# A chunked state-space scan: two heads' M and x in one product, and another order of the turn

## The chip, the cores and the metric

The kernel runs on one core of a Trainium2 chip. The metric is the device time of one execution in microseconds (us). Three executions of the kernel before took 242.53, 243.75 and 241.89, so the median is 242.53.

## The reference

Two blocks follow each other. The first is a Mamba-2 scan over 4 batches, 8 heads and 768 positions, with 32 columns of x a head and a state of 16 x 32. The second sends each of the 3072 tokens to one of 8 experts by a hash of its id.

```python
for c in range(nc):                       # chunks of 32 positions
    L = np.exp(cum[:, :, :, None] - cum[:, :, None, :]) * causal
    M = np.einsum('bhin,bhjn->bhij', Cc, Bc) * L
    y_intra = np.einsum('bhij,bhjd->bhid', M, xc)
    y_inter = np.einsum('bhin,bhnd->bhid', Cc, state) * decay_to_i[:, :, :, None]
    y[:, :, sl] = y_intra + y_inter
    state = decay_full[:, :, None, None] * state + np.sum(Bx, axis=2)
...
x = y.transpose(0, 2, 1, 3).reshape(3072, 256)
for e in range(8):
    out[e's tokens] = np.maximum(x[e's tokens] @ w1[e], 0.0) @ w2[e]
```

The result does not depend on the size of a chunk. The kernel uses chunks of 64.

## The kernel before, in words

**The scan.** The 3072 positions are cut into 12 pairs of 128-position tiles (three pairs a batch, `PB`). Each tile holds two chunks of 64, `u`. A loop (`for k in range(-1, NP)`, L724) runs one *turn* per pair, and works on three pairs at once: it finishes pair k, makes the products of pair k + 1 and prepares pair k + 2. Every engine executes its instructions in exactly the order in which the program writes them; there is no planner (`manual_schedule`, L85), and engines wait for each other by semaphores. The pieces of a turn are:

- `turn_bc` and `evict_bc` (L214, L225): TensorE transposes a third of the next batch's B and C, scaled by the decays, and ScalarE copies the transposes to SBUF as `bt`, `ce` (C, split into even and odd heads) and `ct`. A batch is ready after three turns; the last part of C is turned in turns 1, 4 and 7, and the `gram` of those same turns reads it.
- `back` and `evict_back` (L520, L526): B of pair k + 2 is transposed back, and copied to `bn`.
- `gram` (L566): C times B for each head, chunk and tile of pair k + 2. Each product covers a 32-row, 64-column part of the TensorE array.
- `masked` (L578): VectorE copies the causal half of it to `m_sb`, in two instructions of 128x512.
- `intra` (L611): M times x for pair k + 1, one product for each of 8 heads, 2 tiles and 2 chunks. M of 64x64 is the stationary operand, x of two heads (64 columns) the moving one, and half of each result isn't used. The results go to the PSUM banks `BY` and `BY + 1`. A tiny ScalarE copy, `seen`, follows them.
- `dstates` and `states` (L530, L543): B times x gives each chunk's addition to the state; VectorE chains them as `z`, and GpSimd scales each into `sp`.
- `inter` (L591): C times the state, added to intra's results of pair k in PSUM; then ScalarE evicts y to `y_sb`, and `y_store` (L626) writes it to DRAM.

TensorE's order in a turn is: `turn_bc`, `back`, `inter(k)`, `gram(k + 2)`, `intra(k + 1)`, `dstates(k + 2)`. ScalarE's is: first evictions of B and C, y of pair k, `bn`, the other evictions, `seen`.

**The routing**, in pieces beside the scan (`piece`, L675), finds out which token goes to which slot of an expert. Its last steps need one-hot rows of each tile's lanes (`rt_lanes`, L403): VectorE makes some in a few wide instructions, GpSimd makes the others one by one. In turn 8 TensorE multiplies them into a table (`rt_table`, L419), from which the index lists come.

**The seam.** After the scan GpSimd gathers the tokens' rows in tiles of 128 (`gather`, L474). Tiles 0 to 6 (`EK`) hold only tokens from the first 2048, and are asked for early (`ASK`, L718); the others need all of y in DRAM. `turn_x` (L482) transposes a gathered tile. The experts' products then start with those that need only early tiles: 16 `up` groups of four matmuls (L984 to L1004), between which tiles are turned. In `step(0)` (L1025) follow the other products of expert 0, for which VectorE makes sums and differences of quarters of the matrices (`sum_w1`, `sum_w2`, `sums_x`, L803 to L825), since each expert's product is done with seven products of quarters in place of eight. From there on, to the end, TensorE goes through the eight experts.

Trace records: an fp32 matmul of the program shows as two records on PE and two weight loads on PEld.

Of the kernel before, what the change touches and what calls it, by code (L numbers as in the profile page):

```python
# [25 lines left out]
def kernel(  # L26
# [113 lines left out]
    m_sb = [awork.tile([P, 2, G, 2 * T], F32, name=f"m{i}", bufs=1) for i in range(2)]  # L140
# [4 lines left out]
    cmask = apre.tile([P, 2, T], F32)  # L145
    pool_e.memset(cmask, 1.0)
    for u in range(2):
        pool_e.affine_select(out=cmask[u * T:(u + 1) * T], in_=cmask[u * T:(u + 1) * T], pattern=[[0, 2], [1, T]],
                             compare_op=OP.is_ge, fill=0.0, base=0, channel_multiplier=-1)
# [380 lines left out]
    def dstates(k, bank=0, half=1):  # L530

        b, j = divmod(k, PB)
        for t in range(2):
            for hh in range(2):
                for u in range(2):
                    if j == PB - 1 and t == 1 and u == 1:
                        continue
                    pe.matmul(out=ps[hh * T:(hh + 1) * T, bank + u, half * 2 * P + t * P:half * 2 * P + (t + 1) * P],  # L538
                              lhsT=bns[k][u * T:(u + 1) * T, t, hh * T:(hh + 1) * T],
                              rhs=xs[2 * k + t][u * T:(u + 1) * T, 4 * hh:4 * hh + 4].rearrange("q h d -> q (h d)"),  # L540
                              start=True, stop=True, skip_group_check=True)

    def states(k, ns, bank=0, half=1):  # L543
# [4 lines left out]
        for n in ns:  # L548
# [10 lines left out]
            d = ps[:, bank + u, half * 2 * P + t * P:half * 2 * P + (t + 1) * P]  # L559
# [4 lines left out]
            zs["z"] = z  # L564

    def gram(k):  # L566
        b, j = divmod(k, PB)
        for gs in ((2, 3), (0, 1)):
            for t in range(2):
                for u in range(2):  # L570
                    c = (2 * j + t) * P + u * T
                    for g in gs:
                        r = slice(32 * g, 32 * g + 32)
                        pe.matmul(out=ps[u * T:(u + 1) * T, g, t * P:(t + 1) * P].rearrange("q (e i) -> q e i", e=2),  # L574
# [3 lines left out]
    def masked(k, half):  # L578
        m = m_sb[k % 2]
        mk = cmask.bitcast(I32).rearrange("q e i -> q (e i)").unsqueeze(1).unsqueeze(1).to_broadcast([P, 2, 2, 2 * T])  # L580
        g = slice(2 * half, 2 * half + 2)
        dve.copy_predicated(out=m[:, :, g], mask=mk, data=ps[:, g, 0:2 * P].rearrange("q g (t s) -> q t g s", t=2))  # L582

    def y_own(r, u):

        v = ps[r, BY + u].rearrange("q (t g b d) -> q t g b d", t=2, g=2, d=D)
        return v[:, :, :, 0:4:3]
# [3 lines left out]
    def inter(k):  # L591
# [3 lines left out]
        for u in range(2):  # L595
            for t in range(2):
# [4 lines left out]
                for hh in range(2):  # L601
                    r = slice(hh * T, (hh + 1) * T)
                    pe.matmul(out=y_own(r, u)[:, t], lhsT=cts[b][r, c:c + T], rhs=sps[k][r, n], start=False, stop=True,  # L603
                              skip_group_check=True)
            o = ysb[k].rearrange("q t u (g e d) -> q u t g e d", g=2, e=2)
            if k == NP - 1 and u:
                dve.tensor_copy(out=o[:, u], in_=y_own(slice(0, P), u))
            else:
                act.activation(o[:, u], y_own(slice(0, P), u), AF.Copy)

    def intra(k):  # L611
        for t in range(2):
            for h4 in range(4):
                for u in range(2):
                    for hh in range(2):
                        h = hh * 4 + h4
                        o = ps[hh * T:(hh + 1) * T, BY + u, (t * 4 + h4) * 2 * D:(t * 4 + h4 + 1) * 2 * D]
                        pe.matmul(out=o, lhsT=m_sb[k % 2][u * T:(u + 1) * T, t, h // 2, (h % 2) * T:(h % 2 + 1) * T],  # L618
                                  rhs=xs[2 * k + t][u * T:(u + 1) * T, h // 2 * 2:h // 2 * 2 + 2],
                                  start=t == 0 and h4 == 0, stop=False, skip_group_check=True)  # L620
# [54 lines left out]
    def piece(k):  # L675
# [20 lines left out]
        elif k == 6:  # L696
            rt_tiles()
            rt_lanes(0, 4, dve)
            rt_lanes(15, 18, pool_e)
        elif k == 7:  # L700
            rt_lanes(4, 11, dve)
            rt_lanes(18, NCH, pool_e)
# [15 lines left out]
    ASK = {8: EK[:2], NP - 2: EK[2:-1]}  # L718
# [5 lines left out]
    for k in range(-1, NP):  # L724
# [12 lines left out]
        tb, qb, sb = (BY + 1, BY, BT) if k == -1 else (BT, BQ, 0)  # L737
        if bt_ < NB:
# [11 lines left out]
        if k == NP - 2:  # L750
            for i, q in enumerate(AHEAD):
                turn_x(q, (BQ, BT)[i % 2])
        if k >= 0:
            inter(k)
# [20 lines left out]
        if k == 7:  # L775
            rt_lanes(11, 15, dve)
# [4 lines left out]
        if k == NP - 2:  # L781

            passed = apre.tile([P, 2, 1], F32)
# [34 lines left out]
    def sums_x(p):  # L818
        n = HALF[p]
        q = lambda k, j: xT[:, k, slots(p, j)]  # L820
        t = t1[p] = mwork.tile([P, 4, N0], F32, name="t1")
        dve.tensor_tensor(out=t[:, 0, 0:n], in0=q(0, 1), in1=q(0, 0), op=OP.subtract)  # L822
        dve.tensor_tensor(out=t[:, 1, 0:n], in0=q(1, 1), in1=t[:, 0, 0:n], op=OP.subtract)
        dve.tensor_tensor(out=t[:, 2, 0:n], in0=q(0, 1), in1=q(1, 1), op=OP.subtract)
        dve.tensor_tensor(out=t[:, 3, 0:n], in0=q(1, 0), in1=t[:, 1, 0:n], op=OP.subtract)  # L825
# [153 lines left out]
    ask(2)  # L979
    gather(EK[-1], early=True)  # L980
    ask(4)
    turns = [k for k in EK if k not in turned] + turn_due(0)
    n = 0
    for p in range(NEAR):  # L984
        for what in (1, 2):
            for q0 in (0, 2):
                up(p, q0, what, (0, 1, 2, BT)[(2 * p + q0 // 2) % 4], sts[p, q0])
                n += 1
                if n in (2, 4, 6, 8, 10, 14, 15, 16) and turns:
                    k = turns.pop(0)  # L990
                    turn_x(k, eng=dve if n < 14 else act)
# [33 lines left out]
    def step(p):  # L1025
# [16 lines left out]
        for s in range(max(len(ups), len(downs))):  # L1042
            if s < 4 and p > 0:
                sums_h(p - 1, s)
            for q0, w in ups[s] if ups else ():
                up(p, q0, w, bank_of(p, q0, w), sts[p, q0])
            if turns:
# [27 lines left out]
            if s == (4 if p else 3) and p + 1 < E:  # L1075
# [4 lines left out]
                sums_x(p + 1)  # L1080
# [98 lines left out]
```

## Time and profile before

| | us |
|---|---|
| median of three executions | 242.53 |
| the profiled execution, its own time | 243.41 |
| its span, first to last instruction | 241.7 |
| PE busy | 222.2 (92% of the span) |
| PEld (weight loads) busy | 204.6 |
| VectorE (DVE) busy | 169.8 |
| GpSimd (POOL) busy | 101.5 |
| ScalarE (ACT) busy | 97.3 |

PE is busy in nearly every slice of the span, but a matmul's record includes its latency, so a full slice doesn't mean that no time is lost. The loop's turns begin at 13.7 us (turn -1) and the last product of the scan ends at about 68.7 us; the seam lasts to about 96 us. L618 (`intra`) has 768 records of a 64x64 stationary operand and a 64x64 moving one, L603 (`inter`) 176, L574 (`gram`) 384. The 23 evictions of y on ACT (L609) take 385 ns each in the mean, and one more runs on DVE. A line such as "0.71 <-PE ps L222" gives how long the engine sat idle before an instruction, and what ended that.

### The profile page before, as it was taken

How to read it: one execution, taken by the hardware profiler on the slowest of the kernel's cores; microseconds unless marked ns; L12 is line 12 of the kernel's file. 1: busy time of each engine (PE TensorE's matmuls, PEld its weight loads, DVE VectorE, ACT ScalarE, POOL GpSimd, SP SyncE). 2: the span in 40 equal slices, each digit the busy share in tenths (PEclk: the TensorE clock that was granted, in tenths of full speed). 3: DMA queues.
4: the chain of work that ended last, by engine and by line, in shares of the span. 5: the costliest groups of instructions: out<-in, count | busy, mean ns of one | idle time of the engine just before them, and what ended most of it. 6: DMA issues, size and time to landing. Idle time of an engine off the chain costs nothing.

```text
span 241.7 us, 6845 instructions
## 1 busy us (share of the span) xinstructions
PE 222.2 (92%) x2695; PEld 204.6 (85%) x2695; DVE 169.8 (70%) x351; ACT 97.3 (40%) x249; POOL 101.5 (42%) x179
## 2 busy tenths in 40 slices
PE   7897989998968898999999999999999999999970
PEld 5676778776757787999999999999999999999960
DVE  6687886986515689989979977666839649537520
ACT  4645645652424634213303415525534543542220
POOL 2575879798656771102601551201430420310351
PEclk9999999999999999999999999999999999999995
DMA  7987788786666879303905626503211510610111
GB/s 176 213 170 153 162 177 185 167 175 183 196 179 183 258 240 326 139 0 94 328 15 165 248 92 193 198 3 124 93 40 25 178 43 3 196 43 3 45 52 40
DMA packets 55174, 33.23 MB, mean 137 GB/s; under 512 B 34986, under 2 KB 49474, under 8 KB 55140
## 3 DMA queue, kind: packets, MB, share of 16 engines
q1 hardware_dynamic: 52288, 26.09, 40.2%
q0 software_dynamic: 2400, 6.43, 8.2%
q8 instruction: 22, 0.36, 0.6%
q10 hardware_dynamic: 452, 0.25, 0.4%
q14 instruction: 12, 0.10, 0.1%
HBM read 26.47 MB, written 6.42 MB: 136 GB/s over the span
## 4 chain that ended last, share of the span: by engine, by line
PE 37%; issue 32%; POOL 13%; DVE 8%; DMA 4%; ACT 2%; POOLq 1%; SPq 0%; DVEq 0%; ACTq 0%
PE ps L923 10%; PE ps L864 9%; POOL out_dram L952 9%; PE ps L618 4%; PE ps L574 3%; DMA y_tokens<-y_sb 3%; PE ps L603 3%; PE ps L222 2%; POOL laneoh L406 2%; PE ps L538 2%; DMA xg<-y_tokens,idx_in 1%; DVE s L806 1%; ACT ce L236 1%; PE ps L485 1%; POOL sp L553 1%
## 5 line engine op out<-in xcount | busy, mean ns | idle before, releaser
L952 POOL DMA_INDIRECT out_dram<-o_sb,idx_out x25 | 29.8, 1191 | 73.8 <-ACT o_sb L948 71.2
L477 POOL DMA_INDIRECT xg<-y_tokens,idx_in x25 | 26.1, 1043 | 42.2 <-PE ps L943 30.1
L864 PE MATMUL ps<-t,s 128*128 128x202 f32 (+7 forms) x192 | 38.1, 328 | 0.9 <-DVE hx L901 0.5
L923 PE MATMUL ps<-t,s 128*128 128x202 f32 (+7 forms) x192 | 35.2, 326 | 0.0
L864 PEld LDWEIGHTS ps<-t,s 128*128 128x128 f32 x192 | 32.0, 189 | 2.2 <-DVE t L822 1.0
L923 PEld LDWEIGHTS ps<-t,s 128*128 128x128 f32 x192 | 31.3, 189 | 0.0
L864 PE MATMUL ps<-xT,w 128*128 128x202 f32 (+7 forms) x128 | 25.0, 328 | 0.5 <-DVE xT L489 0.5
L806 DVE TENSOR_TENSOR s<-w 128x512 f32<-128x512 f32 x32 | 21.9, 684 | 0.0
L864 PEld LDWEIGHTS ps<-xT,w 128*128 128x128 f32 x128 | 21.1, 190 | 0.9 <-DVE xT L489 0.8
L553 POOL TENSOR_TENSOR sp<-z,gm 128x128 f32<-128x128 f32 x44 | 18.1, 421 | 8.0 <-DVE z L563 5.4
L897 ACT ACTIVATE hx<-hx 128x404 f32<-128x404 f32 (+7 forms) x16 | 8.4, 527 | 30.3 <-DVE hx L896 30.3
L563 DVE SCALAR_TENSOR_TENSOR z<-z,g_sb,ps 128x128 f32<-128x128 f32 x40 | 13.9, 347 | 6.0 <-PE ps L538 2.2
L582 DVE COPY_PREDICATED m<-cmask,ps 128x512 f32<-128x512 int32 x24 | 16.2, 728 | 2.7 <-PE ps L574 2.6
L618 PE MATMUL ps<-x_t,m 64*64 64x64 f32 x768 | 15.5, 222 | 2.2 <-issue 1.9
L618 PEld LDWEIGHTS ps<-x_t,m 64*64 64x64 f32 x768 | 13.1, 134 | 5.1 <-issue 2.9
L929 ACT ACTIVATE d<-ps 128x202 f32<-128x202 f32 (+7 forms) x24 | 8.0, 333 | 13.9 <-PE ps L923 13.9
L864 PE MATMUL ps<-t,w 128*128 128x202 f32 (+7 forms) x64 | 13.2, 330 | 0.4
L864 PE MATMUL ps<-xT,s 128*128 128x202 f32 (+7 forms) x64 | 12.9, 326 | 0.0
L603 PE MATMUL ps<-sp,ct 64*64 64x128 f32 x176 | 12.2, 276 | 0.4 <-ACT seen L622 0.4
L923 PE MATMUL ps<-t,w 128*128 128x202 f32 (+8 forms) x72 | 12.4, 314 | 0.0
L485 PE MATMUL ps<-ident,xg 128*128 128x128 f32 x50 | 9.6, 277 | 2.6 <-DMA xg<-y_tokens,idx_in 2.6
L923 PE MATMUL ps<-h,w 128*128 128x202 f32 (+7 forms) x64 | 11.8, 326 | 0.0
(178 smaller groups left out, 440.2 us busy)
## 6 DMA issues: line engine op xcount, KB each, us to landing
w<-in_moe_w_dram SPq DMA_DIRECT2D x8, 1024.0 KB, 5.7
w<-in_moe_w_dram SPq DMA_DIRECT2D x11, 512.0 KB, 6.7
x_t<-in_x_dram SPq DMA_DIRECT2D x24, 128.0 KB, 4.0
y_tokens<-y_sb SPq DMA_DIRECT2D x23, 128.0 KB, 3.7
w<-in_moe_w_dram SPq DMA_DIRECT2D x10, 256.0 KB, 3.7
bc<-in_B_dram SPq DMA_DIRECT2D x4, 384.0 KB, 4.6
bc<-in_C_dram SPq DMA_DIRECT2D x4, 384.0 KB, 4.4
xg<-y_tokens,idx_in POOLq DMA_INDIRECT x25, 4.9
```

The source lines that it names most:

```text
L477: pool_e.indirect_dma_start(out=xg[k], out_offset=None, in_=y_dram[0:n, :], in_offset=bass.IndirectOffsetOnAxis(ap=idx_in[:, k:k + 1], axi ...
L485: pe.transpose(out=ps[:, bank, i * P:(i + 1) * P], in_=t[:, i * P:(i + 1) * P], identity=ident)
L553: pool_e.tensor_tensor(out=sps[k][:, n].rearrange("q (h d) -> q h d", d=D), in0=zs["z"].rearrange("q (h d) -> q h d", d=D), in1=gm[:, un - ...
L563: dve.scalar_tensor_tensor(out=z, in0=zs["z"], scalar=g_sb[:, un - 1:un], in1=d, op0=OP.mult, op1=OP.add)
L582: dve.copy_predicated(out=m[:, :, g], mask=mk, data=ps[:, g, 0:2 * P].rearrange("q g (t s) -> q t g s", t=2))
L603: pe.matmul(out=y_own(r, u)[:, t], lhsT=cts[b][r, c:c + T], rhs=sps[k][r, n], start=False, stop=True, skip_group_check=True)
L618: pe.matmul(out=o, lhsT=m_sb[k % 2][u * T:(u + 1) * T, t, h // 2, (h % 2) * T:(h % 2 + 1) * T], rhs=xs[2 * k + t][u * T:(u + 1) * T, h // ...
L806: dve.tensor_tensor(out=t[:, i], in0=a, in1=b, op=op)
L864: pe.matmul(out=ps[:, bank, i * n:(i + 1) * n], lhsT=lhs[:, (q0 + i) * P:(q0 + i + 1) * P], rhs=rhs, start=((what in (1, 5) or what == (6 ...
L897: act.activation(hq(2), hq(2), AF.Relu)
L923: pe.matmul(out=src, lhsT=lhs(q), rhs=rhs(q)[:, c0:c1], start=((what in (1, 5) or alone) and q == 0), stop=True, skip_group_check=True)
L952: st = pool_e.indirect_dma_start(out=out[:], out_offset=bass.IndirectOffsetOnAxis(ap=idx, axis=0), in_=o_sb, in_offset=None, bounds_check= ...
```

## The change

In `intra`, M of heads f and f + 4 lies side by side, so that one stationary operand has 128 columns, and x of the two heads is the moving operand. There are 16 products a pair in place of 32. Each writes 128 rows: those of the lower half that belong to head f, those of the upper half that belong to head f + 4, with the unused half of the columns as before. `m_sb`, the mask, the PSUM places of `gram` and `dstates` and the reading of y follow: y is evicted in two halves of 64 rows and 512 columns rather than two of 128 rows and 256 columns.

In the loop, `inter(k)` with its evictions goes to the head of the turn, and in turn 10 the first two tile transposes with it. GpSimd makes 6 of the 24 lane tiles in place of 9. Three early gathers are issued in turn 8 in place of two, one in turn 9 after a wait for `seen`, three in turn 10; then six follow in a row. Tiles are turned earlier among the 16 `up` groups, and the four `sums_x` of expert 1 are spread over two places.

```diff
-    m_sb = [awork.tile([P, 2, G, 2 * T], F32, name=f"m{i}", bufs=1) for i in range(2)]
+    m_sb = [awork.tile([P, 2, G, 2, T], F32, name=f"m{i}", bufs=1) for i in range(2)]
...
-    cmask = apre.tile([P, 2, T], F32)
+    cmask = apre.tile([P, T], F32)
...
+    def part_of(bank, t):
+        c = (2 * t + 1) * P if bank == 0 else (2 + t) * P
+        return slice(c, c + P)
...
-                    pe.matmul(out=ps[hh * T:(hh + 1) * T, bank + u, half * 2 * P + t * P:half * 2 * P + (t + 1) * P],
+                    pe.matmul(out=ps[hh * T:(hh + 1) * T, bank + u, part_of(bank, t)],
...
+    def bc_at(r, g):
+        return ps[r, g].rearrange("q g (e f t i) -> q (g e) f t i", e=2, f=2, t=2)[:, :, 0]
...
     def masked(k, half):
...
+        mk = cmask.bitcast(I32).unsqueeze(1).unsqueeze(1).to_broadcast([P, 2, G, T])
+        dve.copy_predicated(out=m_sb[k % 2][:, :, :, half], mask=mk,
+                            data=bc_at(slice(0, P), slice(2 * half, 2 * half + 2)).rearrange("q h t i -> q t h i"))
+
+    def y_own(hh):
+        return ps[hh * T:(hh + 1) * T, BY:BY + 2].rearrange("q u (t f b d) -> q u t f b d", t=2, b=2, d=D)[:, :, :, :, hh]
...
-            o = ysb[k].rearrange("q t u (g e d) -> q u t g e d", g=2, e=2)
-            if k == NP - 1 and u:
-                dve.tensor_copy(out=o[:, u], in_=y_own(slice(0, P), u))
+        for hh in range(2):
+            o = ysb[k][hh * T:(hh + 1) * T].rearrange("q t u (f d) -> q u t f d", d=D)
+            if k == NP - 1 and hh:
+                for u in range(2):
+                    dve.tensor_copy(out=o[:, u], in_=y_own(hh)[:, u])
             else:
-                act.activation(o[:, u], y_own(slice(0, P), u), AF.Copy)
+                act.activation(o, y_own(hh), AF.Copy)

     def intra(k):
         for t in range(2):
-            for h4 in range(4):
+            for f in range(G):
                 for u in range(2):
-                    for hh in range(2):
-                        h = hh * 4 + h4
-                        o = ps[hh * T:(hh + 1) * T, BY + u, (t * 4 + h4) * 2 * D:(t * 4 + h4 + 1) * 2 * D]
-                        pe.matmul(out=o, lhsT=m_sb[k % 2][u * T:(u + 1) * T, t, h // 2, (h % 2) * T:(h % 2 + 1) * T],
-                                  rhs=xs[2 * k + t][u * T:(u + 1) * T, h // 2 * 2:h // 2 * 2 + 2],
-                                  start=t == 0 and h4 == 0, stop=False, skip_group_check=True)
+                    pe.matmul(out=ps[:, BY + u, (t * G + f) * 2 * D:(t * G + f + 1) * 2 * D],
+                              lhsT=m_sb[k % 2][u * T:(u + 1) * T, t, f].rearrange("q h i -> q (h i)"),
+                              rhs=xs[2 * k + t][u * T:(u + 1) * T, f:H:G],
+                              start=t == 0 and f == 0, stop=False, skip_group_check=True)
...
-            rt_lanes(0, 4, dve)
-            rt_lanes(15, 18, pool_e)
+            rt_lanes(0, 5, dve)
+            rt_lanes(18, 21, pool_e)
         elif k == 7:
-            rt_lanes(4, 11, dve)
-            rt_lanes(18, NCH, pool_e)
+            rt_lanes(5, 13, dve)
+            rt_lanes(21, NCH, pool_e)
...
-    ASK = {8: EK[:2], NP - 2: EK[2:-1]}
+    ASK = {8: EK[:3], NP - 3: EK[3:4], NP - 2: EK[4:]}
...
         tb, qb, sb = (BY + 1, BY, BT) if k == -1 else (BT, BQ, 0)
+        if k >= 0:
+            inter(k)
+        if k == NP - 2:
+            for i, q in enumerate(AHEAD):
+                turn_x(q, (BQ, BT)[i % 2])
         if bt_ < NB:
             turn_bc(bt_, part, tb)
...
             states(k + 1, (2, 3), sb)
-        if k == NP - 2:
-            for i, q in enumerate(AHEAD):
-                turn_x(q, (BQ, BT)[i % 2])
-        if k >= 0:
-            inter(k)
...
         if k == 7:
-            rt_lanes(11, 15, dve)
+            rt_lanes(13, 18, dve)
...
-        if k == NP - 2:
-            passed = apre.tile([P, 2, 1], F32)
+        if k in (NP - 3, NP - 2):
+            passed = apre.tile([P, 2, 1], F32, name=f"passed{k}")
             pool_e.tensor_copy(out=passed, in_=seen)
...
-    ask(2)
-    gather(EK[-1], early=True)
-    ask(4)
+    ask(6)
...
-                if n in (2, 4, 6, 8, 10, 14, 15, 16) and turns:
+                if n in (1, 2, 5, 7, 9, 12, 13, 14) and turns:
                     k = turns.pop(0)
-                    turn_x(k, eng=dve if n < 14 else act)
+                    turn_x(k, eng=dve if n < 12 else act)
...
                 up(p, q0, w, bank_of(p, q0, w), sts[p, q0])
+                if p == 0 and s == 4:
+                    sums_x(1, (2 + q0 // 2,))
...
-                sums_x(p + 1)
+                sums_x(p + 1, range(4 if p else 2))
```

## The prediction

> **What bounds the kernel now.** I read the page's slices first, then windows cut at the scan's turns, then one turn on each engine in order of time, and last the same for the seam. TensorE is the fullest engine almost everywhere and runs at full clock:
>
> ```profile
> PE   7897989998968898999999999999999999999970
> PEclk9999999999999999999999999999999999999995
> ```
>
> From about 96 us on it never stops and the diff leaves that part alone, so what counts is the scan (13.7 to 68.7 us) and the seam after it (to 96 us). Windows cut where a turn's first PE instruction starts (PE's busy time comes first, then PEld, DVE, ACT, POOL); shown are turns 2, 4, 7, 8 and the seam in two pieces:
>
> ```profile
> 27.23:31.47 4.24, 4.24 (x138) 3.46 (x134) 3.62 (x9) 1.83 (x5) 3.33 (x10) 1.00 0.74 142
> 36.36:40.71 4.35, 4.20 (x136) 3.45 (x134) 3.14 (x7) 2.80 (x8) 4.01 (x10) 1.00 0.77 166
> 49.51:53.87 4.36, 4.22 (x136) 3.47 (x134) 3.50 (x7) 2.80 (x7) 4.36 (x9) 1.00 0.82 180
> 53.87:59.77 5.90, 4.79 (x158) 3.85 (x154) 3.90 (x12) 1.22 (x4) 5.48 (x9) 1.00 0.69 182
> 68.67:85.63 16.96, 13.62 (x81) 11.84 (x79) 7.84 (x16) 8.57 (x22) 12.61 (x13) 1.00 0.72 212
> 85.63:95.98 10.35, 9.69 (x54) 8.74 (x55) 10.06 (x22) 3.06 (x7) 4.75 (x5) 1.00 0.93 297
> ```
>
> An ordinary turn lasts about as long as PE has work in it. Its blocks, turn 2 on PE in order of time:
>
> ```profile
> 27.23 0.66 PE L222 MATMUL ps<-ident,rows 128*128 128x128 f32 x4
> 27.72 0.38 PE L524 MATMUL ps<-ident,bt 128*128 128x128 f32 x2
> 28.03 1.09 PE L603 MATMUL ps<-sp,ct 64*64 64x128 f32 x16
> 29.05 0.72 PE L574 MATMUL ps<-ce,bt 32*64 32x128 f32 x32
> 29.70 1.18 PE L618 MATMUL ps<-x_t,m 64*64 64x64 f32 x64
> 30.88 0.67 PE L538 MATMUL ps<-x_t,bn 64*64 64x128 f32 x16
> ```
>
> Start to start: B/C turns 0.49, back 0.31, inter 1.02, gram 0.65, intra 1.18, dstates 0.59; together 4.24. One wait matters below. In turn 1, ACT and PE go:
>
> ```profile
> 23.36 1.28 ACT L236 ACTIVATE ce<-ps,par 128x512 f32<-128x512 f32 x2 [0.71 <-PE ps L222]
> 24.54 0.65 ACT L609 ACTIVATE y_sb<-ps 128x256 f32<-128x256 f32 x2
> 24.69 0.73 PE L574 MATMUL ps<-ce,bt 32*64 32x128 f32 x32
> ```
>
> In turns 1, 4 and 7 gram needs the C just turned and evicted in that same turn; today ACT does that eviction first, while PE runs inter, and gram starts 0.05 us after it.
>
> **What the Trainium skill says.** "TensorE: Matmul & The Clock Gate", section "LDWEIGHTS (loading the stationary operand)": a load takes the number of columns / 1.2 ns, whatever the number of rows. Two back-to-back pairs of loads agree (weight loads in order of time, 128 columns beside a product of only 48):
>
> ```profile
> 10.37 0.30 PEld L507 LDWEIGHTS ps<-rg,rep 128*128 128x128 f32 x2
> 10.60 0.30 PEld L509 LDWEIGHTS ps<-rg,rep 128*128 128x128 f32 x2
> ```
>
> 0.23 us from pair to pair is 115 ns a load; the product needs only about 41 ns (0.85 ns a column, from 1.37 us for eight of 202). So with few moving columns the load sets the pace. Same page, "Part 3: Packing small matmuls — row/col tiling": tiles of the array load and multiply side by side. The trace agrees for four 64x64 tiles: intra's 64 loads
>
> ```profile
> 29.70 1.04 PEld L618 LDWEIGHTS ps<-x_t,m 64*64 64x64 f32 x64 [0.17 <-ACT y_sb L609]
> ```
>
> come in 16 groups of four; (1.04 - 0.13 of the last load) / 15 = 60 ns a group, which is what one 64-column load (53 ns by the formula) and one product of 64 columns (54 ns) each need. "TensorEngine Tiling (Array Packing)", "Key Properties": a change of tiling mode drains the array. The trace shows 0.2 us there (second back transpose, 0.11 after 31.96, to inter at 32.28, where transposes follow each other by 0.11). Before and after there are four such changes a turn (dstates and the next inter become alike, intra and dstates unlike), so I count nothing.
>
> **The change, part by part.**
>
> *M and x of heads h and h + 4.* Removed: half of intra's records, 64 of 64x64 become 32 of 64x128 a turn. But the groups stay 16: before four tiles at once, now two row tiles (u) at once. No row shows a 64x128 load. Below: 60 ns a pair, if its load is no limit. Above: 224, if the two row tiles load one after the other. I take 112, the 128-column pace with both row tiles side by side, as the four tiles are now. Intra's issue goes from 16 x 60 = 0.96 to 16 x 112 = 1.79: **+0.83 us**, twelve times, on PE's own path. What it covers: the waits at intra's edges for y and bn evictions (0.2 us), so +0.65 net in an ordinary turn.
>
> *y's eviction.* 23 evictions of 128x256 at 385 ns become two a turn of 64x512; the nearest rows are bt and ct of 128x512, 621 and 655. Two issued in a row take about 0.5 + 0.65 = 1.15 us where they took 0.65 to 0.82, and both now wait for all of inter.
>
> *Inter first in the turn.* Its input (POOL's sp) is made a turn earlier, so PE needn't wait. But its y evictions now stand ahead of the B/C evictions in ACT's queue. In turns 1, 4, 7: inter ends at +1.09 (0.82 of issue, 0.27 to the last end), y runs 1.14 to 2.29, the two ce evictions issue from 2.14 and end at about 3.43 (1.28 for both, as above). Gram starts at 3.47; PE is ready at 1.02 + 0.49 + 0.31 = 1.82. Before it started at 24.69 - 22.66 = 2.03. So +1.45 a turn, and behind it wait gram, intra, dstates. This turn: 3.47 + 0.65 + 1.83 + 0.6 = 6.55 against 4.57, 4.35 and 4.36: **+2.0, +2.2, +2.2**.
> Other turns, in the same way: turn -1 +0.6 (intra alone); 0, 3, 6 (twelve inter records) +0.5, +0.5, +0.3; 2 and 5 +0.7, +0.6; 9 +0.6 (gram's second half waits for DVE's four z, some 2.0 us into the turn); 10 +0.9 (two y evictions between inter and intra instead of one and a half, no gram between). Turn 8: below.
>
> *Lanes.* POOL loses 3 of 9 lanes x 596 ns = 1.8 us, DVE gains 3 at about 132 ns (1.08 - 0.68 us for 7 and 4 lanes) = 0.4, in slack (3.5 busy of 4.4). Turn 8's table waited 0.76 for ACT's bn and 0.35 for the last lane. The lane's wait goes; the bn's grows, since bn stands behind two longer y evictions: table at 2.6 instead of 2.2, gram at 3.35 instead of 3.44. With intra, turn 8 is +0.5.
> Sum of the scan: 0.6 + 1.3 + 1.3 + 6.4 + 0.5 + 0.6 + 0.9 = **+11.6**. PE's intra also stands still twice with no releaser (1.22 us in turn 0, 0.68 in turn 3), where PE's instruction queue runs dry as I take it; 768 fewer PE instructions may spare none or both; I take 1.0 off: **+10.6**.
>
> *Token tiles.* Gathers for tiles 2 and 3 move from after the scan to turns 8 and 9, on POOL ahead of states(10) and (11). A gather is 1.0 to 1.3 us plus 0.3; sp of turn 10 is then ready about 0.5 us before inter needs it, that of 11 with 1.6 to spare (turn 9's copy of `seen` holds POOL's queue until intra(10) is done). If that cover goes, the cost is what is missing of it.
> Before, PE waited in the seam for gathers:
>
> ```profile
> 71.84 0.44 PE L485 MATMUL ps<-ident,xg 128*128 128x128 f32 x2 [1.53 <-DMA xg<-y_tokens,idx_in]
> 74.00 0.41 PE L485 MATMUL ps<-ident,xg 128*128 128x128 f32 x2 [0.35 <-DMA xg<-y_tokens,idx_in]
> 80.40 0.41 PE L485 MATMUL ps<-ident,xg 128*128 128x128 f32 x2 [0.72 <-DMA xg<-y_tokens,idx_in]
> ```
>
> From the seam's start: 16 ups x 0.69 + 7 tile turns x 0.22 = 12.6 us of PE in 16.96. After: tile 4 lands at 3.2, wanted at 3.9; 5 at 4.5, wanted at 5.5; 6 at 5.8, wanted at 7.1; 7 and 8 need the last y in DRAM (0.35 later, by the longer evictions): issued at 6.0 and 7.3, landed 3.45 later at 9.45 and 10.75, wanted at 9.4 and 10.35. Waits of 0.45 remain: 13.1 instead of 16.96, **-3.9**. The second half of w1(1) is issued as before at 3.0, lands at 9.5, and its four sums (0.6 each) are ready when PE is.
>
> *Squares of the seam (sums_x).* In 85.63 to 95.98 DVE is the bound (10.06 of 10.35). The four subtractions of tile set 0 (0.3 each) leave that stretch, since DVE does them before PE gets there, and two of set 1 move behind the evictions that PE waited 0.5 us for: **-1.2**, at most what PE idles there now (about 2).
>
> *Nothing for* the mask's shape, PSUM places and m's order: same 512 elements a masked copy (728 ns, DVE has room).
>
> Sum: 10.6 - 3.9 - 1.2 = **+5.5**. The profiled execution took 243.41 (span 241.7 and 1.7 around it), so 248.9 for it; the median shown is 0.9 lower, so **248.0**.
>
> **The rivals.** *Faster:* a 64x128 load isn't the limit and a pair takes 60 ns. Then 12 x 0.83 goes, less some 0.7 where z, masks or y hold PE instead: 248.0 - 9.2 = 238.8. It decides between 112 and about 66 ns (where 5.5 us are gone). For it: nothing in the trace shows this tile shape; against: L507. *Loads in turn:* 224 ns a pair, +21.5: 269.5; against it four loads within 60 ns today. *The seam's gain doesn't come* (gathers land late while DMA is 0.72 to 0.93 busy): 253.1. *Gram isn't delayed* (y and C don't queue as I say): 3 x 1.45 less, 243.6, no change.
>
> **The numbers.** Forecast 0.65 (own range 244.5 to 252: instruction stalls, 1 us; the waits, 2; the seam, 2), faster 0.16, loads in turn 0.05, no seam gain 0.08, no delay 0.06. A measurement of this kernel can tell about 1% from no change. Slower by over 1%: 0.92 x 0.65 + 0.05 + 0.08 = 0.73; faster 0.15; within 0.12. The range takes in the faster rival's half and the missing seam gain's: 239.0 to 253.5.
>
> **What would show it.** L618: 384 records, weight loads near 190 ns, 1.8 us from its first to dstates. Turns 1, 4, 7 near 6.5 us, with PE idle over 1 us before gram for ACT's ce. y evictions of 64x512 near 0.65. No wait for tiles 2 and 3 in the seam, 16 ups in about 13 us. I am wrong if intra issues in 1 us, if gram in turn 1 starts by 2.2 us, or if turns grow by less than 0.4 us.

## The result, and the profile after

The changed kernel takes 259.49 us (median of four executions, 259.19 to 262.04), the kernel before 242.8 beside it: a ratio of 1.071, 95% interval 1.063 to 1.079. The change makes the kernel slower, as forecast, but by 16.7 us where +5.5 was worked out; 259.5 lies outside the range of 239.0 to 253.5.

| | before | after |
|---|---|---|
| the profiled execution | 243.41 | 259.37 |
| its span | 241.7 | 257.7 |
| the scan's last product ends | 68.7 | 88.1 |
| the 16 `up` groups with their tiles | 16.96 | 13.97 |
| the piece after them, to the first product of `w2` | 10.35 | 9.75 |

So the scan lost 19.4 us, where 10.6 was expected, and the seam with the squares won 3.6, where 5.1 was expected. I first read the slices of the page of the changed kernel:

```profile
PE   8898998899779899999999999999999999999990
PEclk9999589679799999999999999999999999999995
```

The second row is what this kernel has and the one before had not: in three places of the scan TensorE is granted about half of its clock. Windows cut at the turns show which turns (turns 0, 1, 2, 4, 5, 7, 8, and the seam; after the length come the busy times of PE, PEld, DVE, ACT and POOL, then the mean granted clock, the DMA share and GB/s):

```profile
17.66:22.67 5.01, 5.01 (x103) 4.38 (x95) 3.95 (x8) 3.28 (x9) 2.85 (x5) 1.00 0.87 188
22.67:31.63 8.96, 7.17 (x106) 6.37 (x104) 3.64 (x9) 3.39 (x7) 3.68 (x9) 0.73 0.89 182
31.63:37.44 5.81, 5.81 (x109) 5.04 (x103) 3.71 (x9) 2.23 (x5) 3.62 (x10) 0.82 0.16 41
42.44:50.83 8.39, 6.59 (x106) 5.89 (x104) 3.13 (x7) 3.40 (x7) 5.55 (x12) 0.79 0.67 138
50.83:57.24 6.41, 6.41 (x108) 5.47 (x103) 3.88 (x11) 2.24 (x5) 2.71 (x5) 0.74 0.33 81
62.24:70.02 7.78, 5.98 (x106) 5.29 (x104) 4.23 (x7) 3.40 (x7) 5.35 (x10) 0.86 0.56 124
70.02:77.14 7.12, 5.78 (x128) 5.11 (x123) 3.38 (x11) 1.74 (x4) 2.77 (x5) 0.92 0.43 104
88.09:102.06 13.97, 13.46 (x80) 11.99 (x79) 9.16 (x19) 8.89 (x21) 9.28 (x10) 1.00 0.68 191
```

Turn 0, at full clock, is shorter than before (5.01 us; 5.45 before, with the stall of 1.22 in it). Turns 1, 4 and 7 and those behind them (2, 5 and 8) are too long, and they are the ones with a clock below 1. Turn 1 of the changed kernel in order of time, ACT first:

```profile
23.80 1.21 ACT L618 ACTIVATE y_sb<-ps 64x512 f32<-64x512 f32 x2 [1.27 <-PE ps L610]
25.03 1.28 ACT L236 ACTIVATE ce<-ps,par 128x512 f32<-128x512 f32 x2
```

and PE:

```profile
24.18 0.38 PE L524 MATMUL ps<-ident,bt 128*128 128x128 f32 x2
26.36 0.83 PE L583 MATMUL ps<-ce,bt 32*64 32x128 f32 x32 [1.79 <-ACT ce L236]
27.12 3.68 PE L624 MATMUL ps<-x_t,m 64*128 64x64 f32 x32
30.73 1.13 PE L543 MATMUL ps<-x_t,bn 64*64 64x128 f32 x16
```

The wait that was predicted is there: y's two evictions, then the two of ce, and `gram` 3.69 us into the turn (3.47 predicted). But `intra` (L624) then takes 3.68 us, and in turn 0 only 2.00 for the same 32 products. Windows laid on the edges of the low clock, with the 3.41 us ahead of each:

```profile
23.44:26.85 3.41, 1.62 (x44) 1.20 (x40) 1.93 (x6) 3.01 (x6) 3.31 (x9) 1.00 0.94 186
26.85:33.67 6.82, 6.82 (x84) 6.11 (x66) 2.67 (x7) 0.46 (x3) 1.49 (x6) 0.50 0.66 143
43.92:47.33 3.41, 1.61 (x46) 1.20 (x44) 1.05 (x3) 2.88 (x6) 3.20 (x8) 1.00 0.75 160
47.33:54.16 6.83, 6.83 (x65) 6.05 (x62) 3.23 (x8) 1.48 (x4) 3.58 (x7) 0.50 0.31 61
64.40:67.81 3.41, 1.88 (x54) 1.71 (x55) 1.50 (x3) 2.21 (x5) 3.19 (x6) 1.00 0.60 145
67.81:71.22 3.41, 3.41 (x42) 3.29 (x42) 1.67 (x4) 0.17 (x1) 0.40 (x2) 0.50 0.04 14
```

Three times the clock is halved, for 6.83, 6.83 and 3.41 us, each time at the end of a window in which PE was busy for about half of the time: 17.07 us at half speed, in which at most 8.5 us of work didn't get done. The scan's excess over the forecast is of that size (8.8). The Trainium skill, "TensorE: Matmul & The Clock Gate", section "Part 1: The HAM clock gate (the "warmup" mystery)", describes this: TensorE's clock is full or half, decided by how busy it was in a free-running window of 3413 ns. The trace agrees in the halving and in the window: the three starts lie 20.48 us apart, six times 3.413, and each stretch is one or two windows long. The same page, "HAM oscillation — how this bites in real kernels", puts the danger at gaps of PE over about 3.4 us; there the measurement differs, since pauses of 1.79 us were followed by half clock.

The new `intra` itself is as predicted. Its weight loads in turn 0:

```profile
20.24 1.86 PEld L624 LDWEIGHTS ps<-x_t,m 64*128 64x128 f32 x32 [0.17 <-issue]
```

(1.86 - 0.19 for the last load) / 15 = 111 ns from pair to pair: the two row tiles load side by side, and the 128 columns set the pace.

### The profile page after: what moved, and what is told of

It is laid out like the page before. It is cut to its first block, busy times and chain, and to the rows that moved or that the text cites. A ratio compares the mean times of both kernels' runs of the same rounds, so it can differ in the third digit from the quotient of the medians.

```text
span 257.7 us, 6082 instructions
## 1 busy us (share of the span) xinstructions
PE 239.1 (93%) x2311; PEld 222.5 (86%) x2311; DVE 170.4 (66%) x352; ACT 102.7 (40%) x249; POOL 100.0 (39%) x177
## 4 chain that ended last, share of the span: by engine, by line
PE 50%; issue 28%; POOL 8%; DVE 5%; ACT 5%; POOLq 1%; ACTq 0%; DVEq 0%
PE ps L872 11%; PE ps L624 10%; PE ps L931 9%; POOL out_dram L960 8%; PE ps L610 5%; PE ps L583 4%; PE ps L543 3%; PE ps L175 3%; ACT y_sb L618 3%; PE ps L222 2%; ACT ce L236 2%; DVE s L813 1%; PE ps L485 1%; PE ps L524 1%; DVE u L900 1%
## 5 line engine op out<-in xcount | busy, mean ns | idle before, releaser
L624 PEld LDWEIGHTS ps<-x_t,m 64*128 64x128 f32 x384 | 25.7, 211 | 3.0 <-issue 1.3
L624 PE MATMUL ps<-x_t,m 64*128 64x64 f32 x384 | 27.5, 300 | 0.7 <-ACT y_sb L618 0.7
L618 ACT ACTIVATE y_sb<-ps 64x512 f32<-64x512 f32 x23 | 13.6, 592 | 18.2 <-PE ps L610 17.9
L583 PE MATMUL ps<-ce,bt 32*64 32x128 f32 x384 | 10.6, 282 | 6.1 <-ACT ce L236 5.4
L583 PEld LDWEIGHTS ps<-ce,bt 32*64 32x64 f32 x384 | 7.3, 131 | 8.8 <-ACT ce L236 6.1
L610 PE MATMUL ps<-sp,ct 64*64 64x128 f32 x176 | 14.4, 309 | 0.4 <-ACT seen L629 0.4
```

The source lines that it names most:

```text
L583: pe.matmul(out=bc_at(slice(u * T, (u + 1) * T), slice(g, g + 1))[:, :, t], lhsT=bts[b][r, c:c + T], rhs=ces[b][r, :, c:c + T], start=True ...
L610: pe.matmul(out=y_own(hh)[:, u, t], lhsT=cts[b][r, c:c + T], rhs=sps[k][r, n], start=False, stop=True, skip_group_check=True)
L618: act.activation(o, y_own(hh), AF.Copy)
L624: pe.matmul(out=ps[:, BY + u, (t * G + f) * 2 * D:(t * G + f + 1) * 2 * D], lhsT=m_sb[k % 2][u * T:(u + 1) * T, t, f].rearrange("q h i -> ...
```

## The experiments

The theory now: the change makes a pause of 1.8 us before `gram` in turns 1, 4 and 7, and after it TensorE runs at half clock, which costs some 8 us on its own. The rival: the long turns are the waits and the loads alone, and the clock is a sign of them, not a cause. The runs below were made in three groups, each on one chip with the kernel before beside it (249.6 us on the first chip, 242.6 and 242.1 on the other two), so ratios to the kernel before are compared, and times only within a group.

**Keep TensorE busy in the wait.** 28 products of zeros, in bf16, go into the pause, and write to PSUM columns that nothing reads. Nothing else differs from the changed kernel.

```diff
+        if k in (1, 4, 7):
+            for _ in range(28):
+                pe.matmul(out=ps[:, 3, P:2 * P], lhsT=fill16[:, 0:P], rhs=fill16[:, 0:P], start=True, stop=True,
+                          skip_group_check=True)
         if k + 2 < NP:
             gram(k + 2)
```

First on the first chip:

> The changed kernel, with 28 products of zeros (bf16, 128x128x128[...]) put on PE ahead of gram in turns 1, 4 and 7, where PE idled 1.8 us for ACT's ce. The waits stay as long as they are. Theory A (the pause makes the chip grant half the clock for 17.1 us, which costs 8.5): no drop, 259.5 - 8.5 = 251. Theory B (the clock falls because products paced by their loads leave the array half unused, pause or not): drops stay, about 259.

Measured: 1.049 (1.042 to 1.057). The clock stayed full in turns 1 to 8, and these were 7.45 us shorter than in the changed kernel's trace, which is from another chip; but it fell at the ends of turns 9 and 10 instead, after windows in which PE was idle for only 0.7 and 0.9 us. The first of these windows, and the one behind it:

```profile
72.23:75.64 3.41, 2.73 (x46) 2.32 (x48) 2.19 (x5) 1.56 (x3) 1.03 (x3) 1.00 0.53 122
75.64:79.05 3.41, 3.41 (x36) 2.96 (x35) 1.04 (x3) 0.34 (x2) 2.06 (x5) 0.50 0.47 153
```

These two falls fit theory B of the expectation (products paced by their loads bring the clock down, pause or not) better than theory A; they come back under what stays open. As the time alone proved little, the changed kernel and the one with the filler were then run together, on the second chip:

> The changed kernel again, on the chip of the other three runs, so that they can be compared with it. Theory (half-speed clock after the pause before gram in turns 1, 4 and 7): ratio to the kernel before 1.05 to 1.08, with the clock at half after those three pauses, some 17 us in all. Rival (the long turns are only waits and loads): no fixed place of the low clock.

> The changed kernel with 28 bf16 products of zeros before gram in turns 1, 4 and 7, beside the changed kernel on the same chip. Theory: the clock stays full in turns 1 to 8, and these are 7 to 8.5 us shorter; the time is 5 to 8 us less than the changed kernel's (less if the clock falls in a later turn). Rival (waits and loads alone): no more than 1 us from the changed kernel, since the filler only fills a wait that stays as long.

Measured: the changed kernel 1.0744 (1.067 to 1.082), with the filler 1.0388 (1.0335 to 1.044). By these ratios, adding 84 products took off 3.6% of 242.6, or 8.6 us; the two traced executions, 257.79 and 251.12, differ by 6.7 us, and in that of the changed kernel the clock fell after two pauses and not three. The changed kernel's four executions took 257.8, 259.1, 262.0 and 266.9 us, at mean clocks of 0.964, 0.958, 0.941 and 0.927: the time follows the clock. The slices of the page of the run with the filler:

```profile
PEclk9999999999999999999999999999999999999997
```

and its turn 1 on PE:

```profile
24.38 1.73 PE L774 MATMUL ps<-fill 128*128 128x128 bf16 x28
26.34 0.73 PE L583 MATMUL ps<-ce,bt 32*64 32x128 f32 x32 [0.23 <-ACT ce L236]
27.00 2.00 PE L624 MATMUL ps<-x_t,m 64*128 64x64 f32 x32
```

`gram` starts as late as before (26.34 against 26.36), so the wait has not been shortened; only `intra` behind it is back at 2.00. The rival is out: it allowed 1 us. Theory B is out as the only cause, too: the merged products are all there, and the clock is full.

The changed kernel on that chip gave a control that I had not planned. Its three pauses are equal, but in turn 1 the clock did not fall (`gram` of the three turns, PE in order of time):

```profile
26.35 0.73 PE L583 MATMUL ps<-ce,bt 32*64 32x128 f32 x32 [1.79 <-ACT ce L236]
43.17 1.19 PE L583 MATMUL ps<-ce,bt 32*64 32x128 f32 x32 [1.80 <-ACT ce L236]
62.97 0.73 PE L583 MATMUL ps<-ce,bt 32*64 32x128 f32 x32 [1.79 <-ACT ce L236]
```

Windows of the same run, counted back in steps of 3.413 us from the two falls, for turns 1 and 4, each with what followed it:

```profile
22.78:26.19 3.41, 1.77 (x24) 1.36 (x21) 2.31 (x7) 2.35 (x5) 2.71 (x6) 1.00 0.91 182
26.20:29.60 3.40, 3.25 (x84) 2.98 (x86) 1.34 (x2) 1.03 (x4) 0.95 (x4) 1.00 0.83 172
39.85:43.26 3.41, 1.61 (x28) 1.21 (x27) 1.61 (x5) 2.61 (x5) 3.05 (x8) 1.00 0.73 140
43.26:50.09 6.83, 6.83 (x93) 6.38 (x95) 2.04 (x5) 0.80 (x3) 2.61 (x6) 0.50 0.49 97
```

An edge at 26.19 cut 0.16 us off turn 1's pause. What was left in its window, 1.64 us of idle time, was not enough; 1.79 was. (In turn 7 of the first trace, where the rest of the window was `gram` and the merged `intra`, 1.53 was enough, so idle time alone doesn't draw the line.) The grid lies differently from execution to execution, so one and the same pause is followed by 3.4 or 6.8 us of half clock in one execution, and by none in another.

**A pause by itself.** The kernel before, with ce's first copy repeated ahead of itself, so that PE only waits:

```diff
         elif bt_ < NB:
+            for _ in range({1: 2, 4: 3, 7: 5}.get(k, 0)):
+                evict_bc(bt_, part, tb, (None, act))
             evict_bc(bt_, part, tb, (act, act, None if part == 1 else act, None))
```

> The kernel before, with the first copy of ce repeated ahead of itself 2 times in turn 1, 3 times in turn 4 and 5 times in turn 7 (the same values again, 0.64 us each), so that gram waits about 1.3, 1.9 and 3.2 us and nothing else is changed. Theory (a pause makes the clock fall): no fall after turn 1's, half speed for 3.4 or 6.8 us after turn 4's and turn 7's; 6.4 us for the pauses and 3.4 to 7 for the low clock, together 10 to 13 us, ratio 1.04 to 1.055. Rival (a pause costs its length): 6.4 us, ratio 1.026, and the clock full throughout.

Measured: 1.035 (1.030 to 1.040), between the two. The pauses were 1.59, 2.33 and 3.77 us, and only the last was followed by half clock (`gram` in order of time):

```profile
25.21 0.73 PE L574 MATMUL ps<-ce,bt 32*64 32x128 f32 x32 [1.59 <-ACT ce L236]
40.77 0.73 PE L574 MATMUL ps<-ce,bt 32*64 32x128 f32 x32 [2.33 <-ACT ce L236]
57.41 1.19 PE L574 MATMUL ps<-ce,bt 32*64 32x128 f32 x32 [3.77 <-ACT ce L236]
```

Windows of this run on its own grid, the two that share turn 4's pause, then turn 7's and the one behind it:

```profile
36.16:39.57 3.41, 2.28 (x34) 1.70 (x26) 2.08 (x6) 2.23 (x4) 3.16 (x10) 1.00 0.69 182
39.58:42.98 3.40, 2.21 (x112) 1.97 (x112) 1.34 (x2) 2.63 (x7) 2.69 (x5) 1.00 0.55 100
53.23:56.64 3.41, 0.41 (x8) 0.17 (x4) 0.93 (x1) 3.28 (x5) 3.41 (x7) 1.00 0.68 136
56.64:63.47 6.83, 6.06 (x128) 5.07 (x130) 3.24 (x7) 2.58 (x8) 3.51 (x8) 0.50 0.30 79
```

So a pause alone does it, with the old products and the old order. My expectation was wrong on turn 4: its 2.33 us lay across an edge, 1.13 in one window and 1.20 in the next, and neither was idle enough. In this run the idle time in one window decided, not the length of the pause. Turns 1 and 4 grew by 1.2 and 2.2 us, a little less than their pauses; turn 7 by 5.2 with a pause of 3.8, as the rest of it ran at half speed. The pause that did it took 3.0 us of its window; that 1.8 us are enough without the merged product is shown by the run with the squares below.

**The load pace alone.** In the changed kernel `intra` is written as 64x64 products again, on the new layout; with the filler, and on the first chip without it.

```diff
-                    pe.matmul(out=ps[:, BY + u, (t * G + f) * 2 * D:(t * G + f + 1) * 2 * D],
-                              lhsT=m_sb[k % 2][u * T:(u + 1) * T, t, f].rearrange("q h i -> q (h i)"),
+                    for hh in range(2):
+                        pe.matmul(out=ps[hh * T:(hh + 1) * T, BY + u, (t * G + f) * 2 * D:(t * G + f + 1) * 2 * D],
+                                  lhsT=m_sb[k % 2][u * T:(u + 1) * T, t, f, hh],
```

> The filler, and intra as 64 records of 64x64 instead of 32 of 64x128, on the changed layout and order. Both theories give intra 0.8 us less in each of 12 turns where the clock is full, so 8 to 10 us less than with the filler alone. What is left of the scan's loss against the kernel before should then be the gram waits of turns 1, 4 and 7, 1.5 to 2 us each.

Measured: 1.0103 (1.007 to 1.014), against 1.0388 with the filler alone: 2.85% or 6.9 us (6.1 between the traced executions), less than the 8 to 10 expected. Both traces are at full clock, and the scan's end moved from 80.6 to 74.4, 0.51 us a turn; PE now stands still for 0.2 to 0.5 us with no releaser in several turns, as in the kernel before, which the longer products had covered. Turns 1, 4 and 7 take 5.96, 5.97 and 5.96 us with nothing left of the change in them but the wait (4.57, 4.35 and 4.36 before).

> The changed kernel, with intra's products as 64x64 squares again (32 a pair, same layout, same order of the turn). Theory A: intra issues in 1.0 instead of 1.8 us, which is 12 x 0.83 = 10 at full clock, but the pauses before gram in turns 1, 4 and 7 stay and the clock still falls there: 249 to 250. Theory B: with squares the clock stays full, 259.5 - 8.5 - 10 = 241.

Measured: 1.032 (1.027 to 1.038). The waits before `gram` were 1.82, 1.81 and 1.80 us, and the clock fell after the first two: the low clock doesn't need the new products. The third was cut by an edge into 0.43 and 1.37 us, and the clock stayed full. It fell twice more, at 70.1 and 97.4 us, the latter after waits of the seam (0.45 and 1.92 us with no releaser) whose cause is open.

**What makes the pause.** Two parts stand ahead of ce's evictions: the order (inter and y first) and the layout (y in two evictions of 64x512, which both need all of inter). First the order alone, on the kernel before:

```diff
+        if k >= 0:
+            inter(k)
+        if k == NP - 2:
+            for i, q in enumerate(AHEAD):
+                turn_x(q, (BQ, BT)[i % 2])
         if bt_ < NB:
             turn_bc(bt_, part, tb)
...
-        if k == NP - 2:
-            for i, q in enumerate(AHEAD):
-                turn_x(q, (BQ, BT)[i % 2])
-        if k >= 0:
-            inter(k)
         if k + 2 < NP:
             evict_back(k + 2, qb)
```

> The kernel before with inter(k) and its two y evictions at the head of the turn (and the two tile transposes of turn 10 with it), the layout of M, the lanes and the seam as before. The y evictions of 128x256 take 0.65 to 0.82 us for two instead of 1.2, so gram in turns 1, 4 and 7 should start at about +3.2 and wait 1.2 to 1.4 us for ce. Theory: that is near the edge, so the clock falls after none or some of them: 3 to 4 us for the waits, 0 to 10 for the clock, ratio 1.012 to 1.055. Rival (the order costs only with the new layout): ratio under 1.01.

Measured: 1.0074 (1.003 to 1.012): below the theory's range, and in that of the rival (under 1.01). Without the new layout the order costs little; in the trace the scan ends at 68.5, where it ended at 68.7 before. The waits, 1.15 to 1.16 us, were a little shorter than expected, and the clock stayed full after all three. Turn 1 of this run, ACT in order of time:

```profile
22.23 0.82 ACT L609 ACTIVATE y_sb<-ps 128x256 f32<-128x256 f32 x2 [1.05 <-PE ps L603]
23.24 1.28 ACT L236 ACTIVATE ce<-ps,par 128x512 f32<-128x512 f32 x2 [0.19 <-PE ps L222]
```

and PE:

```profile
24.57 0.73 PE L574 MATMUL ps<-ce,bt 32*64 32x128 f32 x32 [1.16 <-ACT ce L236]
```

Here the first y eviction starts 0.76 us after inter does, when half of inter is done; in the changed kernel 1.13, and ce follows 1.23 later instead of 1.01. These 0.6 us are what the layout adds, from 1.16 to 1.79, and they carry the pause into the region where the clock falls. Turns 1, 4 and 7 grew by 2.6 us together, and turns 0 (4.4 in place of 5.5) and 8 (5.2 in place of 5.9) gave 1.8 of it back, others the rest.

Then, in the changed kernel, y's evictions moved behind those of ce in turns 1, 4 and 7:

```diff
+        late = j == 1 and bt_ < NB
         if k >= 0:
             inter(k)
+            if not late:
+                y_evict(k)
...
+        if late:
+            y_evict(k)
         if k + 1 < NP:
             states(k + 1, (2, 3), sb)
```

> The changed kernel, with the two y evictions of turns 1, 4 and 7 put behind the two ce evictions on ACT; all else as changed. Theory A: gram starts about 2.1 us into the turn, no pause, no drop of the clock: 259.5 - 8.5 - 3 x 1.7 = 246. Theory B: only the waits go, 254.5, with half clock still in places. If the weight loads cost nothing, 240 or less.

Measured: 1.057 (1.050 to 1.065), little better than the changed kernel (1.071 and 1.074 on the other chips; it wasn't run on this one), and worse than either forecast (246 or 254.5 us, 1.3% or 4.8% over 242.8). The wait before `gram` fell only to 1.15 us, since C is turned on PE behind inter and ACT can't evict it before that; and `intra` then waited 0.35 for y. The clock stayed full in turns 1 and 4, but fell in turn 7 and twice more before the end of the scan, after windows with only 1.50, 0.45 and 0.87 us of idle time.

**The merged product alone.** The kernel before with the new `intra`, its layout and y's halves; order, lanes and seam stay as they were. Its core:

```diff
-                        pe.matmul(out=o, lhsT=m_sb[k % 2][u * T:(u + 1) * T, t, h // 2, (h % 2) * T:(h % 2 + 1) * T],
-                                  rhs=xs[2 * k + t][u * T:(u + 1) * T, h // 2 * 2:h // 2 * 2 + 2],
+                    pe.matmul(out=ps[:, BY + u, (t * G + f) * 2 * D:(t * G + f + 1) * 2 * D],
+                              lhsT=m_sb[k % 2][u * T:(u + 1) * T, t, f].rearrange("q h i -> q (h i)"),
+                              rhs=xs[2 * k + t][u * T:(u + 1) * T, f:H:G],
```

> The merged product alone, with the layout and the 64x512 y evictions that it needs; order of the turn, lanes, gathers, token tiles and sums as in the kernel before. Theory A: no pause before gram, so full clock, and 0.65 net in each of twelve intras: 242.8 + 7.8 = 250.6. Theory B: half clock in places, 255 and more.

Measured: 1.053 (1.045 to 1.062). Turns last 5.5 to 5.7 us; `intra` waits 0.45 to 0.63 in nearly each for y's eviction, which now stands right ahead of it. And the clock falls here too, in turns 8 and 10, behind windows with 1.33 and 1.31 us of idle time, and once in the seam (PE in order of time):

```profile
66.15 0.77 PE L422 MATMUL ps<-tab,laneoh 128*128 128x50 bf16 x24 [1.71 <-ACT bn L528]
67.50 3.05 PE L624 MATMUL ps<-x_t,m 64*128 64x64 f32 x32
...
80.52 2.46 PE L624 MATMUL ps<-x_t,m 64*128 64x64 f32 x32 [1.31 <-ACT y_sb L618]
83.40 1.97 PE L610 MATMUL ps<-sp,ct 64*64 64x128 f32 x16 [0.42 <-ACT seen L629]
```

So taking back the order doesn't save the product: with its layout alone it costs 5%. Theory A had forecast full clock here, and theory B what was measured; 17.07 us at half clock account for at most 8.5 of the 13.3 us.

**The seam alone.** Lanes, gathers, token tiles and squares of the change, on the kernel before; of the edits, all as in the change:

```diff
-    ASK = {8: EK[:2], NP - 2: EK[2:-1]}
+    ASK = {8: EK[:3], NP - 3: EK[3:4], NP - 2: EK[4:]}
...
-                if n in (2, 4, 6, 8, 10, 14, 15, 16) and turns:
+                if n in (1, 2, 5, 7, 9, 12, 13, 14) and turns:
...
-                sums_x(p + 1)
+                sums_x(p + 1, range(4 if p else 2))
```

> The kernel before with only the lanes, the gathers, the token tiles' places and the squares of the seam from the change. The prediction gave -3.9 for the token tiles and -1.2 for the squares: 5.1 us less than the kernel before. From the trace of the changed kernel I expect 3.0 and 0.7: ratio 0.98 to 0.99. Rival (the seam's gain comes only because the longer scan gives the gathers time): ratio 1.00, with waits for gathers of 2 us in the seam.

Measured: 0.9934 (0.990 to 0.997), but this ratio takes in only the seven shorter of 20 executions (239.7 to 242.3 us). The other 13 took 243.3 to 246.0, and the median of all, 244.05, lies above the 242.6 of the kernel before: as it stands, this part alone is no sure gain. The seam itself did better than in the changed kernel (13.34 us; 13.97 there, 16.96 before), but in the traced execution (one of the 13, so these waits need not stand in all) the two tile transposes of turn 10 came before their rows, and behind them the clock was at half for 3.4 us (PE in order of time):

```profile
64.66 0.44 PE L485 MATMUL ps<-ident,xg 128*128 128x128 f32 x2 [2.18 <-DMA xg<-y_tokens,idx_in]
66.33 0.44 PE L485 MATMUL ps<-ident,xg 128*128 128x128 f32 x2 [1.23 <-DMA xg<-y_tokens,idx_in]
66.70 1.77 PE L603 MATMUL ps<-sp,ct 64*64 64x128 f32 x16
```

GpSimd had waited 4.0 us for y's store before it could issue the first of the three gathers. So I moved the two transposes behind `intra(11)`, where PE waits 0.4 us for `seen` anyway:

```diff
-        if k == NP - 2:
-            for i, q in enumerate(AHEAD):
-                turn_x(q, (BQ, BT)[i % 2])
         if k >= 0:
             inter(k)
...
             dstates(k + 2)
+        if k == NP - 2:
+            for i, q in enumerate(AHEAD):
+                turn_x(q, (BQ, BT)[i % 2])
```

> The lanes, gathers, token tiles and squares of the change on the kernel before (the run called seam alone), with the two tile transposes of turn 10 moved behind intra(11), where they wait for no gather and lie in PE's wait for seen. The waits of 2.2 and 1.2 us that were seen there should go, and with them the fall of the clock at 67 us: 3.5 to 5 us less than the seam alone, ratio to the kernel before 0.975 to 0.985. Rival (the gathers' time is given back in the seam): ratio 0.99 to 1.00, with waits for gathers in the seam.

Measured: **0.986 (0.982 to 0.990)**, 238.41 us where the kernel before takes 242.11: 1.4% faster than the kernel before, just outside the range expected (0.975 to 0.985), and its four executions lie within 2 us. The end of the scan and the start of the seam on PE, in order of time:

```profile
63.56 1.58 PE L618 MATMUL ps<-x_t,m 64*64 64x64 f32 x64
65.08 0.66 PE L485 MATMUL ps<-ident,xg 128*128 128x128 f32 x4
65.66 1.09 PE L603 MATMUL ps<-sp,ct 64*64 64x128 f32 x16
66.68 0.95 PE L865 MATMUL ps<-xT,w 128*128 128x202 f32 x4
```

No wait is left between `intra(11)` and the seam, and none for a gather in it: 13.34 us, and 9.81 for the piece after it. The traced execution is 6.1 us shorter than that of the kernel before (3.6 in the seam, 0.5 behind it, 2.0 in the scan), but it is the shortest of its four and the two come from different chips; the ratio stands for 3.4 us. In this execution GpSimd also waited only 1.4 us for y's store before the first gather, where it had waited 4.0, so the move of the transposes isn't the only difference between the two traces.

Last, the same with turn 7's loads of x behind the store of y on SP's queue:

```diff
-            if 8 <= c < NCH:
+            if 8 <= c < NCH and k != 7:
                 load_x(c)
...
             y_store(k)
+        if k == 7:
+            load_x(22)
+            load_x(23)
```

> As the run with the tiles late, and in turn 7 the two loads of x are issued behind y's store on SP's queue in place of ahead of it, since the gathers of turn 8 waited 4 us for that store. If this matters, the gathers of turn 8 start 1 to 3 us earlier and the time is less spread, 0 to 1 us less; if not, the same time within 0.3%.

Measured: 0.985 (0.978 to 0.992), no difference from the run before it. But the edit didn't do what it was meant to: the first gather started at 57.26 us, behind a wait of 1.38 for a load of x, where it had started at 57.00. Whether an earlier gather would gain anything is not shown.

## Why the prediction was wrong

- **Loads of 128 columns: right.** 112 ns a pair was taken, 111 measured. By the two runs at full clock the products cost 6.9 us by the ratios and 6.1 by the traces; the prediction's share is 12 x 0.65 - 1.0 for the stalls = 6.8. The rivals "faster" (60 ns) and "loads in turn" (224 ns) are both out.
- **Gram's wait: right in place, short in size.** `gram` starts 3.69 us into turns 1, 4 and 7, where 3.47 was worked out. The first eviction of y starts at 1.13 as worked out (1.14), but ce's evictions start at 2.36 in place of 2.14, since y's follow each other by 0.61 us, not 0.5.
- **The step that failed** is the one that turns this wait into time: "This turn: 3.47 + 0.65 + 1.83 + 0.6 = 6.55". It prices `gram`, `intra` and `dstates` behind the pause by rows of the kernel before, at full clock. With the clock held up by the filler the three turns take 6.78 each, and the scan ends at 80.6: +11.9 where +10.6 was predicted. Without it they take 8.96, 8.39 and 7.78. A pause of PE was taken to cost its length. The row `PEclk` of the kernel before was read as "runs at full clock", and the prediction didn't ask what keeps it there.
- **Lanes and turn 8: right.** 6.57 us at full clock where 6.40 was worked out; the wait for the last lane is gone, and that for `bn` grew from 0.76 to 1.33.
- **Token tiles: -3.0, not -3.9.** The waits for late gathers that were predicted (0.45) didn't come in the changed kernel's trace. Two others did, 0.36 and 0.15 us for an eviction and a tile's copy on their way, and of what is left an `up` took 0.75 us in the mean in place of 0.69. In the run with the tiles late the 16 ups took 13.34 us, against 13.1 predicted.
- **Squares: -0.6, not -1.2**, in the changed kernel, and the same in four other runs with them (9.75 to 9.81 in place of 10.35); in the run with the filler on the first chip this piece took 12.98.
- **Instruction stalls: half counted.** Both are gone, 1.9 us, where 1.0 was taken off.

With the clock full, then, the prediction's sum stands at 8.3 by the traces (11.9 - 3.0 - 0.6) where 5.5 was worked out, within its own range; the measured ratio for that case is 1.0388, +9.4. The other 7 to 9 us are the clock. The range could not hold them, since no case of the prediction had a pause that costs more than its length.

What stays open is what the hardware counts. On the 3.413-us grids of the 14 traces lie 939 windows in which the clock was full, and half clock followed 19 of them (idle time counted as in the windows above). In the eight kernels whose `intra` is made of 64x64 squares it followed the six windows with 1.81 us of idle time or more, and none of the others, in which PE was idle for at most 1.60. In the six kernels with the merged product it followed five windows with 1.79 or more, but also eight with only 0.45 to 1.53, and not three with 1.64 to 1.75, two of them between full 128x128 products of the seam. So theory B has a part in it: beside the merged product, shorter waits were enough. If each product is counted by the rows and columns of the array that it uses and by its moving columns (bf16 as half of fp32), the 19 are among the 31 windows with the least work; by idle time they are only among the 118 with the most. That a product counts by the part of the array that it uses would fit all of this; it was not tried by itself.

## What to carry to other kernels

When a change makes TensorE wait for some 1.8 us within 3.4 in the middle of small products (here less, beside products that wait for their loads), price the work behind the wait at half speed too, for one or two windows of 3.4 us; look at the granted clock by windows before looking for a slow engine, and if the wait can't be removed, fill it with products nobody needs (splitting it in two was not tried). Fewer, wider products are no gain when the moving side is short: at 64 moving columns the 128-column load sets the pace. Before a transfer is blamed, see whether its consumer can move: two transposes that had waited 3.4 us in one trace were put behind the next block, and no longer waited.

## What the runs showed of the hardware that was not expected

- TensorE's clock was halved after each pause of 1.79 us or more that fell within one window of a 3.41-us grid of the scan, and came back after 3.41 or 6.83 us; a pause of 2.33 us across an edge (1.13 and 1.20) did nothing.
- In kernels with the merged product the clock also fell after windows with 0.45 to 1.53 us of idle time; in those with 64x64 squares, never after 1.60 or less.
- 84 bf16 products of zeros, 62 ns each, made a kernel 6.7 to 8.6 us faster: products of zeros count as work.
- Where the grid lies differs between executions, so the same pause can cost up to 3.4 us (half of 6.83) beyond its length in one and nothing in another.
